# Reordering the head of a packed-attention, MoE and soft-MoE kernel, with some PSUM copies and subtractions moved to VectorE

## The chip, the cores and the metric

The kernel runs on one core of a Trainium2 chip. The metric is the device time of one execution in microseconds (us). Three timed runs of the kernel before took 532.25, 533.50 and 533.76 us; their median is 533.5 us. Five engines work side by side, each through its own queue in the order in which the program put the instructions there: PE (TensorE, matrix products), DVE (VectorE), ACT (ScalarE), POOL (GpSimd) and SP (SyncE, which here only issues DMA transfers). An instruction that waits holds up everything behind it on its own engine.

## The reference

The reference chains three layers, all in float32:

```python
# attention with 32 packed queries p per head (batch 4, 8 heads, 576 tokens, head size 64)
p_packed = softmax(scale * p @ k.T) @ v
x = softmax(scale * q @ p_packed.T) @ p_packed          # heads side by side: x is 2304 x 512
# MoE: 4 experts, hidden size 1024, weights dp = domain_probs / row sum
y = sum_e dp[:, e] * (relu(x @ w1[e]) @ w2[e])
# soft MoE: 8 experts with 4 slots each
logits = y @ phi
d, c = softmax(logits, over tokens), softmax(logits, over slots)
out = c @ [ relu((d.T @ y)[e] @ m1[e]) @ m2[e] for each expert e ]
```

## The kernel before

**What is multiplied.** The kernel never forms x or y. With `a` the second softmax of the attention (per token 8 heads times 32 packed keys, laid as 128 rows x 576 tokens for each of the two groups of heads g) and G = p_packed @ w1 (tile `g`, one 256-wide block of hidden units for two experts), the hidden layer of an expert is relu(G.T @ a): `mm1`, L477, tiles `h` and `ht`. Both factors are split into a rounded part and a rest ("hi" and "lo", type fp32r), and hi\*hi + hi\*lo + lo\*hi is accumulated: six products of 128x128 by 128x288 for each half of the tokens. The logits come straight from `ht` with wphi = w2 @ phi (L504, tile `lg`), so all of w2 has to be turned and multiplied with phi once before the first logits.

**The main loop.** There are 16 blocks n (4 batches times 4 blocks of 256 hidden units) and 8 slots for each block, one for each half block and expert. A slot runs its steps in the order F, G, L, M, S, A, P, slots 0 to 3 with M ahead of L: turn the last slot's `ht` (DVE L487) and weight it (POOL L488), now and then make the next G, the slot's `h` products and their relu (ACT L481), logits, softmax, a step of the next batch's attention, pooling. From the second batch on the attention is spread over the loop. The last third of the time streams the weights of the soft MoE and multiplies them.

**The head.** The first batch's attention and the work on w2 have no loop to hide in, and the string `HEAD` lays them out by hand: each character emits one step. `0` and `1` take the next step of the attention of head group g=0 or g=1 (generator `attention`, from one `yield` to the next), `w` the next step of `wphi_steps`, `G` makes one G block (`make_g`, L447 to L459). A `w` step turns two 128-row blocks of w2 for one expert: eight PE transposes (tile `w2t`, L255, four for each block) into one of two PSUM tiles, and a copy of each back over the weights (L260, on ACT for both since `EV` is "00"). After four such steps (one pair of blocks, "fp" 0 to 3) come 32 products with phi (tile `pw`, L241), at the start of the next `w`. The two last steps take `pw` to `wphi` (`wpt`, `wps`, L269 to L275). After the string the rest of both attentions, `norm_probs` (the row sums of domain_probs, a dozen small DVE instructions) and a second `G` follow, then slot 0; slots 0 to 3 take `WG` = 2 further `w` steps each.

**The end of an attention.** A group's softmax `nat` is turned to `a2` rows by DVE (L404), then split, twice (once for each r): ACT rounds 64 rows to "hi" (L413), and `gp` subtracts to "lo" (L414). `gp` is DVE for g=0 and POOL for g=1. `a2_t[0][0]` ("a2_00") and `a2_t[0][1]` ("a2_01") get half of their rows from each group, so the first `h` needs both groups.

**Buffers.** `h`, `g` and score tiles take four PSUM tiles in turn, `w2t` and `wps` two. In the head, g=1 takes its turned tiles ("kt") from the pool of the later `ht` tiles (4 buffers), and its `ex` and `nat` from the second half of the G buffers (`gt[1]`).

Of the kernel before, what the change touches and what calls it, by code (L numbers as in the profile page):

```python
# [9 lines left out]
F32 = mybir.dt.float32  # L10
F32R = mybir.dt.float32r
AF = mybir.ActivationFunctionType
ALU = mybir.AluOpType
# [5 lines left out]
def tile_packed_attention_moe_softmoe(  # L19
# [15 lines left out]
    pe, act, dve, pool, sp = nc.tensor, nc.scalar, nc.vector, nc.gpsimd, nc.sync  # L35

    NB, H, S, D = q.shape
# [19 lines left out]
    PIECES = ((0, 6), (6, 12), (12, 18))  # L57
    ENDS = ((0, 4), (4, 8), (8, 12), (12, 16), (16, 18))
    OFF1 = 9
    HEAD = "000101001011w1001w0011w10w0w1100w10w0101w1w1Gwww10w1G10w"  # L60
    LOADS = "PKkvaqVbQcXd1Wn2W3"
    WARM = 16
    WG = 2
    FILL = 3
    FILL_AT = 1
    EV = "00"
    GP1 = "pool"
    ORDER = "FGLMSAP"

# [83 lines left out]
    def run_due():  # L153
        todo, due[:] = due[:], []
        for f in todo:
            f()
# [67 lines left out]
    def w2_row(ft, e):  # L224
        o = DM * (2 * e + ft % 2)
        return hn_flat[:, PLACE[0][ft // 2], o : o + DM]
# [8 lines left out]
    def wphi_steps():  # L235
        pw = [ps_lg.tile([128, 512], F32, tag="lg", name=f"pw{i}") for i in range(2)]

        def project(ft):
            for dc in range(NDC):
                for e in range(NE):  # L240
                    pe.matmul(  # L241
                        pw[ft // 4][32 * e : 32 * e + 32, 128 * (ft % 4) : 128 * (ft % 4) + 128],
                        phi_sb[:, dc, :],
                        w2_row(ft, e)[:, 128 * dc : 128 * dc + 128],
                        start=(dc == 0),
                        stop=(dc == NDC - 1),
                        tile_position=(0, 32 * e),
                    )

        for fp in range(NFT // 2):  # L250
            for e in range(NE):
                for ft in (2 * fp, 2 * fp + 1):
                    ps = tr_ps(f"w2t_{ft}_{e}")
                    for dc in range(NDC):
                        pe.transpose(  # L255
                            ps[:, 128 * dc : 128 * dc + 128],
                            w2_row(ft, e)[:, 128 * dc : 128 * dc + 128],
                            ident,
                        )
                    (dve.tensor_copy if EV[ft % 2] == "1" else act.copy)(  # L260
                        w2_row(ft, e), ps
                    )
                yield
            project(2 * fp)
            project(2 * fp + 1)
        yield
        for i in range(2):
            wt = sx(f"wpt{i}", [128, 512])
            (dve.tensor_copy if i else act.copy)(wt, pw[i])  # L269
            ps = tr_ps(f"wps{i}")  # L270
            for j in range(4):
                pe.transpose(
                    ps[:, 128 * j : 128 * j + 128], wt[:, 128 * j : 128 * j + 128], ident
                )
            (act.copy if i else dve.tensor_copy)(  # L275
                wphi[:, 4 * i : 4 * i + 4, :].rearrange("p a b -> p (a b)"), ps
            )
            yield
# [3 lines left out]
    def attention(b, g, feeds, ptb, pkb, etb, tmp, gp):  # L282
# [24 lines left out]
        for h in range(4):  # L307
            r = slice(32 * h, 32 * h + 32)
            dve.transpose(
                out=ptb[r, :, 32 * h : 32 * h + 32],  # L310
                in_=pn[r].rearrange("p (j d) -> p j d", j=2),
            )
        kt = [flip(qkv_t.pop(("k", b, g, 0)), "k", 0)]
# [5 lines left out]
        for hf in range(2):  # L319
            ps = scores(ptb, kt[hf], f"sa{bg}{hf}")  # L320
# [16 lines left out]
        for hf in range(2):  # L337
            for h in range(4):
                r = slice(32 * h, 32 * h + 32)
# [40 lines left out]
        for hf in range(2):  # L380
            ps = scores(pkb, qt[hf], f"sb{bg}{hf}")
# [28 lines left out]
        for r in range(2):  # L410
            rows = slice(64 * ((r + g) % 2), 64 * ((r + g) % 2) + 64)
            hi, lo = a2_t[b][r][rows, 0], a2_t[b][r][rows, 1]
            act.copy(hi, a2[rows])  # L413
            gp.tensor_tensor(out=lo, in0=a2[rows], in1=hi.bitcast(F32), op=ALU.subtract)  # L414
        yield

    def att_tmp(tag, name):
# [353 lines left out]
    with tc.manual_schedule():  # L771
# [45 lines left out]
        pp1 = gt[0][:, :256].rearrange("p (j m) -> p j m", j=2)  # L817
        et1 = gt[0][:, 512 : 512 + 2 * S].rearrange("p (r x m) -> p r x m", r=2, m=64)
        spare = {"ex": gt[1][:, :S], "nat": gt[1][:, S : 2 * S]}
        et_x = []  # L820
        for g in range(2):
            et_x.append(a2_pool.tile([128, 2, HB, 64], F32, tag="a2", name=f"etx{g}"))
# [5 lines left out]
        load_probs()  # L828

        def head_tmp(tag, name):  # L830
            if tag == "kt":
                return ht_pool.tile([128, S], F32, tag="ht", name=name)
            return spare[tag]
# [9 lines left out]
        ng = 0  # L843
# [23 lines left out]
                pool_slots(*post.pop(0))  # L867
                limit -= 1

        for e in range(ng, 2):  # L870
            make_g(0, e)
            run_due()

        def finish_wphi():
            for _ in wgen:
# [2 lines left out]
        for sl in range(nslot + 1):  # L878
            n, r = divmod(sl, 8)
            pr, (kf, el) = r // 4, divmod(r % 4, 2)  # L880
            e = 2 * pr + el
            b, i = divmod(n, NU)
            run = sl < nslot
            if not run:
                slots.extend([(a2_pool, "a2", None)] * 2)
                slots.extend([(g_pool, "g", i) for i in range(2)])
                fill_stream()
            run_due()
            if run and b + 1 < NB:
                if sl % 32 == 0:  # L890
                    att_gens.append(start_attention(b + 1, 0))
                if sl % 32 == OFF1:
                    att_gens.append(start_attention(b + 1, 1))
            def step_attention():
                for gen in list(att_gens):
                    if next(gen, "end") == "end":
                        att_gens.remove(gen)
                        if b + 2 == NB and not att_gens and sl % 32 > OFF1:
                            att.close()
                            open_stream("s1", "right")  # L900
                if sl == (NB - 1) * NU * 8:
                    slots.extend([(a2_pool, "a2", None)] * 2)
                if sl == (NB - 1) * NU * 8 + 10:
                    assert not post
                    for k in range(NBLK // XC):
                        ring_slots(k, (0,))
                if sl % FILL == FILL_AT or sl > nslot - 8:
                    fill_stream(sp, 1)

            def step_softmax():  # L910
                nonlocal sm_gen, ready, soon
                ready += soon
                soon = 0
                if sm_gen is not None:
                    st = next(sm_gen, "end")
                    if st == "dp":
                        soon = 1
                    elif st == "end":
                        sm_gen = None

            def step_flip():
                if prev is not None:
                    flip_h(*prev)

            def step_g():
                if not run or r % 4:
                    return
                gn, ge = (n + 1, 0) if r else (n, 1)
                if sl and gn < NB * NU:
                    make_g(gn, ge)  # L930
                    if (gn, ge) == (NB * NU - 1, 1):
                        run_due()
                        slots.extend([(w1_pool, "w1", i) for i in (0, 1, 0, 1)])

            def step_mm():
                if run:
                    mm1(n, kf, e)
                    if n == NB * NU - 1 and kf == 1 and e == 1:
                        slots.extend([(g_pool, "g", i) for i in range(2)])

            def step_logits():
                nonlocal sm_gen, sm_last
                if sl < 4:
                    for _ in range(WG):
                        next(wgen, None)
                if lgq and lgq[0][0] < sl:
                    if sl == 4:
                        finish_wphi()
                    _, ln, lk = lgq.pop(0)
                    logits(ln, lk)  # L950
                    if ln == NB * NU - 1 and lk == 0:
                        sm_last = softmaxes(NB - 1)
                        next(sm_last)
                    if ln % NU == NU - 1 and lk == 1:
                        sm_gen = sm_last if ln == NB * NU - 1 else softmaxes(ln // NU)

            prev, flq = flq, (n, kf, e) if run else None
            steps = {
                "A": step_attention, "S": step_softmax, "F": step_flip, "G": step_g,
                "M": step_mm, "L": step_logits, "P": lambda: run_post(1),  # L960
            }
            for key in "FGMLSAP" if sl < 4 else ORDER if run else "LSFAP":
                steps[key]()
            if run and r % 4 == 3:
                lgq.append((sl, n, pr))
                if b and r == 3 and i == 0:
                    post.extend((b - 1, m) for m in range(len(PIECES)))
# [224 lines left out]
```

## Time and profile before

| | before |
|---|---|
| median of 3 runs | 533.5 us |
| the profiled execution's own time | 533.42 us |
| span of its instructions | 531.6 us |
| PE busy | 493.3 us (93%) |
| DVE / ACT / POOL busy | 292.7 / 236.0 / 248.3 us |
| mean granted TensorE clock | 0.976 of full |
| moved by DMA | 104.06 MB |

The profiled execution's time is 1.8 us more than the span, which runs from its first to its last instruction; it lies within the three timed runs. Times in the rows count from the start of the span. A row of a timeline tells when a group of equal instructions started, how long the group took, how many there were, and in brackets how long the engine was idle just before and who ended that. The granted clock (PEclk) is 1.00 at 2.4 GHz and 0.50 at 1.2 GHz.

### The profile page before, as it was taken

To read this page: it belongs to the slowest core of one execution; us is meant where nothing else is said; L and a number is where in the kernel's file an instruction comes from. 1 tells how busy PE (TensorE), PEld (TensorE's weight loads), DVE (VectorE), ACT (ScalarE), POOL (GpSimd) and SP (SyncE) were. 2 spreads that over 40 slices of the span, in tenths; PEclk is the share of its full clock that TensorE was granted. 3 is DMA by queue.
4 is the path that set the end of the run, shared out by engine and by line. 5 is a ranking of instruction groups with operands and counts; after the bars stand their busy time and mean duration, and the time that the engine had idled before them with its cause. 6 is when DMAs were issued, how large, how long until landed. Compare 5 with 4: busy or idle time off the path is not lost.

```text
span 531.6 us, 12920 instructions
## 1 busy us (share of the span) xinstructions
PE 493.3 (93%) x5404; PEld 349.0 (66%) x5404; DVE 292.7 (55%) x539; ACT 236.0 (44%) x539; POOL 248.3 (47%) x310
## 2 busy tenths in 40 slices
PE   6898999999999999999999999999999987998883
PEld 5776877778765677787557778865678864323232
DVE  6265566656677656567775755676554553412031
ACT  3847555664552447465424474652355430111031
POOL 8502356487752367875326567842455540300000
PEclk9899999999999999999999999999999998898996
DMA  8999135433440353443304423443359449999998
GB/s 276 367 373 315 46 103 191 161 126 127 140 144 3 106 190 105 148 157 104 104 1 150 146 82 129 150 170 109 121 187 390 173 167 373 408 408 407 373 317 282
DMA packets 66713, 104.06 MB, mean 196 GB/s; under 512 B 4368, under 2 KB 50192, under 8 KB 66656
## 3 DMA queue, kind: packets, MB, share of 16 engines
q1 hardware_dynamic: 62640, 93.10, 49.5%
q0 software_dynamic: 3232, 9.75, 6.0%
q8 instruction: 42, 0.69, 0.5%
q10 hardware_dynamic: 784, 0.39, 0.3%
q14 instruction: 15, 0.12, 0.1%
HBM read 98.52 MB, written 4.72 MB: 194 GB/s over the span
## 4 chain that ended last, share of the span: by engine, by line
PE 66%; DMA 11%; DVE 8%; ACT 8%; issue 3%; POOL 3%; SPq 1%; POOLq 0%; DVEq 0%; ACTq 0%
PE h L477 32%; PE sl L648 7%; PE lg L504 6%; PE g L447 5%; DMA ck<-in_moe_w_dram 5%; DMA hn<-in_moe_w_dram 3%; ACT etm L340 3%; PE pv L350 3%; PE sb L301 3%; PE sa L301 2%; DMA k<-in_k_dram 2%; PE w2t L255 1%; PE si L1027 1%; PE o L1153 1%; POOL hn L488 1%
## 5 line engine op out<-in xcount | busy, mean ns | idle before, releaser
L477 PE MATMUL h<-a,g 128*128 128x288 f32 x1536 | 226.2, 302 | 2.5 <-POOL a L414 1.6
L477 PEld LDWEIGHTS h<-a,g 128*128 128x128 f32 x1536 | 208.0, 188 | 28.3 <-issue 22.3
L488 POOL TENSOR_TENSOR hn<-hn,dp_sb 128x576 f32<-128x576 f32 x128 | 151.5, 1190 | 123.0 <-DVE hn L487 118.7
L481 ACT ACTIVATE ht<-h 128x288 f32<-128x288 f32 x256 | 103.7, 412 | 149.4 <-PE h L477 149.0
L487 DVE STREAM_TRANSPOSE hn<-ht 128x576 f32<-128x576 f32 x128 | 96.6, 760 | 55.1 <-ACT ht L481 55.0
L459 DVE TENSOR_TENSOR g<-g,g 128x512 fp32r<-128x512 f32 x64 | 41.1, 684 | 26.5 <-ACT g L458 26.5
L648 PE MATMUL sl<-hn,dpt 32*32 32x512 f32 x1152 | 48.1, 597 | 1.5 <-DVE dpt L607 1.2
L458 ACT CAST g<-g 128x512 fp32r<-128x512 f32 x64 | 34.3, 588 | 21.0 <-PE g L447 21.0
L504 PE MATMUL lg<-ht,wphi 128*32 128x288 f32 x512 | 37.8, 412 | 0.0
L447 PE MATMUL g<-w,gl 64*32 64x512 f32 x512 | 35.7, 601 | 0.2 <-DVE tacc L666 0.2
L648 PEld LDWEIGHTS sl<-hn,dpt 32*32 32x32 f32 x1152 | 21.0, 103 | 21.5 <-issue 11.1
L504 PEld LDWEIGHTS lg<-ht,wphi 128*32 128x32 f32 x512 | 13.5, 109 | 32.7 <-issue 25.5
L350 PE MATMUL pv<-etm,v 128*64 128x64 f32 x468 | 20.0, 232 | 7.1 <-ACT etm L340 4.0
L414 POOL TENSOR_TENSOR a<-a,a 64x576 fp32r<-64x576 f32 x14 | 19.9, 1425 | 9.6 <-ACT a L413 8.9
L350 PEld LDWEIGHTS pv<-etm,v 128*64 128x64 f32 x468 | 17.1, 144 | 11.1 <-ACT etm L340 5.7
L340 ACT COPY etm<-et 32x288 f32<-32x288 f32 x52 | 22.2, 428 | 2.4 <-DVE et L334 1.2
L1120 PE MATMUL so<-hn,tacc 128*32 128x384 f32 (+1 forms) x96 | 19.5, 487 | 2.5 <-DMA hn<-in_moe_w_dram 2.4
L382 DVE STREAM_TRANSPOSE nat<-sb 128x288 f32<-128x288 f32 x14 | 6.8, 483 | 25.4 <-PE sb L301 25.4
L255 PE MATMUL w2t<-ident,hn 128*128 128x128 f32 x128 | 19.3, 301 | 1.4 <-ACT hn L260 1.4
L666 DVE TENSOR_TENSOR tacc<-sl,tacc 128x512 f32<-128x512 f32 (+2 forms) x32 | 15.3, 544 | 9.4 <-PE sl L648 9.4
L260 ACT COPY hn<-w2t 128x512 f32<-128x512 f32 x32 | 17.4, 588 | 6.8 <-PE w2t L255 6.8
L255 PEld LDWEIGHTS w2t<-ident,hn 128*128 128x128 f32 x128 | 15.8, 154 | 5.9 <-ACT hn L260 3.8
(179 smaller groups left out, 483.6 us busy)
## 6 DMA issues: line engine op xcount, KB each, us to landing
w<-in_moe_w_dram SPq DMA_DIRECT2D x32, 1024.0 KB, 5.3
ck<-in_moe_w_dram SPq DMA_DIRECT2D x44, 512.0 KB, 8.9
hn<-in_moe_w_dram SPq DMA_DIRECT2D x40, 512.0 KB, 9.9
hn<-in_moe_w_dram SPq DMA_DIRECT2D x16, 384.0 KB, 8.4
q<-in_q_dram POOLq DMA_DIRECT2D x12, 288.0 KB, 3.2
k<-in_k_dram POOLq DMA_DIRECT2D x10, 288.0 KB, 3.3
v<-in_v_dram POOLq DMA_DIRECT2D x10, 288.0 KB, 3.2
out_dram<-ob SPq DMA_DIRECT2D x7, 384.0 KB, 4.4
```

The lines of the kernel that those rows point to most:

```text
L255: pe.transpose(ps[:, 128 * dc : 128 * dc + 128], w2_row(ft, e)[:, 128 * dc : 128 * dc + 128], ident,)
L340: act.copy(etb[hf % len(etb)][r, h % 2, :, 32 * (h // 2) : 32 * (h // 2) + 32], et[r, HB * hf : HB * hf + HB, :],)
L350: pe.matmul(pv[64 * par : 64 * par + 64, :64], vn[:, x, :], etb[hf % len(etb)][:, par, x, :], start=(hf == 0 and x == 0), stop=(hf == 1 an ...
L447: pe.matmul(pss[g][32 * ((c + 2 * g) % 4) : 32 * ((c + 2 * g) % 4) + 32, :], gl[b % 2][r, c, :], t[r, c], start=True, stop=True, tile_posi ...
L458: act.copy(hi, pss[g])
L459: dve.tensor_tensor(out=lo, in0=pss[g], in1=hi.bitcast(F32), op=ALU.subtract)
L477: pe.matmul(ps[:, :HS], gg[:, l, g, e % 2, fs], r[:, ts], start=(g == 0 and t == 0), stop=(g == 1 and t == 2),)
L481: act.activation(out=ht[:, ts], in_=ps[:, :HS], func=AF.Relu)
L487: dve.transpose(out=own, in_=unturned.pop((n, kf, e)).rearrange("p (x t) -> p x t", t=32))
L488: pool.tensor_tensor(out=own, in0=own, in1=dp_sb[:, n // NU, :, e].unsqueeze(2).to_broadcast([128, NBLK, 32]), op=ALU.mult,)
L504: pe.matmul(lg_t[b, pr][32 * c : 32 * c + 32, :HS], wphi[:, 2 * i + kf, 32 * e : 32 * e + 32], ht_t[n, kf, e][:, HS * hf : HS * hf + HS], ...
L648: pe.matmul(pss[f][c : c + 32, :], dpt[r, x, :], hn[r, p0 : p0 + NU, x, 2 * ep : 2 * ep + 2].rearrange("p n e k f -> p n (e k f)"), start= ...
```

## The change

- `HEAD`: the first step of the ending of g=0 (its casts) is emitted right after its turning (`0` instead of `w` near the end: `...w01w1Gww11w`), and the string stops earlier. The last three `w` steps of the string are left to slots 0 to 3, which take two each as before.
- The second `G` of block 0 is no longer made before slot 0 but in slot 1, in the step G, ahead of that slot's `h` products.
- Of the copies of `w2t` for w2's third pair of blocks (numbers 8 to 11 in the count 4\*fp + e, that is fp = 2), the odd block goes to DVE, the even one stays on ACT.
- The subtraction for `a2_00` is on DVE for both groups in batch 0; that for `a2_01` of g=1 stays on POOL.
- The first turned k tile of g=1 goes to a free part of `gt[1]` instead of an `ht` buffer.

```diff
-    HEAD = "000101001011w1001w0011w10w0w1100w10w0101w1w1Gwww10w1G10w"
+    HEAD = "000101001011w1001w0011w10w0w1100w10w0101w01w1Gww11w"
-    EV = "00"
+    EV_SPLIT = range(8, 12)
...
-                    (dve.tensor_copy if EV[ft % 2] == "1" else act.copy)(
-                        w2_row(ft, e), ps
-                    )
+                    split = ft % 2 and 4 * fp + e in EV_SPLIT
+                    (dve.tensor_copy if split else act.copy)(w2_row(ft, e), ps)
...
-            gp.tensor_tensor(out=lo, in0=a2[rows], in1=hi.bitcast(F32), op=ALU.subtract)
+            (dve if not b and r == 0 else gp).tensor_tensor(
+                out=lo, in0=a2[rows], in1=hi.bitcast(F32), op=ALU.subtract
+            )
...
+        spare_kt = [gt[1][:, 2 * S : 3 * S]]
...
+            if tag == "kt" and spare_kt:
+                return spare_kt.pop()
...
-        for e in range(ng, 2):
-            make_g(0, e)
-            run_due()
...
             def step_g():
+                if sl == 1:
+                    make_g(0, 1)
```

On PE the place is the stretch behind the last turning of w2's third pair of blocks (`w2t_4` and `w2t_5`). Before, in the program's order; `h0_0_0` is the first slot, `g0_1` the second G of block 0 (eight rows of it, two shown):

```order
L255 MATMUL w2t_5_3_652<-ident_103,hn_118 128x128 x4
L241 MATMUL pw1_280<-hn_118,tacc_108 32x128 x32
L255 MATMUL w2t_6_0_698<-ident_103,hn_118 128x128 x4
L255 MATMUL w2t_7_0_704<-ident_103,hn_118 128x128 x4
L447 MATMUL g0_1_0_715<-w1_0_1_166,gl0_113 32x512
L447 MATMUL g0_1_1_716<-w1_0_1_166,gl0_113 32x512
...
L255 MATMUL w2t_6_1_731<-ident_103,hn_118 128x128 x4
L255 MATMUL w2t_7_1_737<-ident_103,hn_118 128x128 x4
L477 MATMUL h0_0_0_0_757<-a2_00_660,g0_0_605 128x288 x3
L477 MATMUL h0_0_0_0_757<-a2_01_661,g0_0_605 128x288 x3
```

The same engine and place after the change:

```order
L255 MATMUL w2t_5_3_663<-ident_103,hn_118 128x128 x4
L478 MATMUL h0_0_0_0_683<-a2_00_555,g0_0_610 128x288 x3
L478 MATMUL h0_0_0_0_683<-a2_01_556,g0_0_610 128x288 x3
L478 MATMUL h0_0_0_1_691<-a2_00_555,g0_0_610 128x288 x3
L478 MATMUL h0_0_0_1_691<-a2_01_556,g0_0_610 128x288 x3
L241 MATMUL pw1_279<-hn_118,tacc_108 32x128 x32
L255 MATMUL w2t_6_0_731<-ident_103,hn_118 128x128 x4
L255 MATMUL w2t_7_0_737<-ident_103,hn_118 128x128 x4
```

The first slot's `h` now stands ahead of `pw`, of the first two experts of w2's last pair of blocks, and of the second G.

On DVE the place is between the end of g=0's attention (`a20`) and `norm_probs` (`dps`). Before:

```order
L404 STREAM_TRANSPOSE a20_539<-nat0_434 128x576
L389 TENSOR_REDUCE bm1_541<-gt1_201 128x18
L396 TENSOR_REDUCE bm1_541<-gt1_201 128x18
L397 TENSOR_SCALAR bm1_541<-bm1_541 128x18
L398 RECIPROCAL bm1_541<-bm1_541 128x18
L459 TENSOR_TENSOR g0_0_605<-g0_0_0_606,g0_0_605 128x512
L459 TENSOR_TENSOR g0_0_605<-g0_0_1_607,g0_0_605 128x512
L404 STREAM_TRANSPOSE a21_658<-gt1_201 128x576
L414 TENSOR_TENSOR a2_00_660<-a20_539,a2_00_660 64x576
L414 TENSOR_TENSOR a2_01_661<-a20_539,a2_01_661 64x576
```

The same stretch of DVE after the change, from the reduction behind `a20`'s turning:

```order
L388 TENSOR_REDUCE bm1_540<-gt1_201 128x18
L413 TENSOR_TENSOR a2_00_555<-a20_538,a2_00_555 64x576
L413 TENSOR_TENSOR a2_01_556<-a20_538,a2_01_556 64x576
L261 COPY hn_118<-w2t_5_0_600 128x512
L395 TENSOR_REDUCE bm1_540<-gt1_201 128x18
...
L460 TENSOR_TENSOR g0_0_610<-g0_0_1_612,g0_0_610 128x512
L261 COPY hn_118<-w2t_5_1_633 128x512
L261 COPY hn_118<-w2t_5_2_645 128x512
L403 STREAM_TRANSPOSE a21_651<-gt1_201 128x576
L413 TENSOR_TENSOR a2_00_555<-a21_651,a2_00_555 64x576
L261 COPY hn_118<-w2t_5_3_663 128x512
```

The subtractions of g=0 moved up, the turning of g=1 (`a21`) now stands behind three copies of `w2t_5`, and its first subtraction follows it on the same engine.

On ACT the same stretch after the change, from the exponential of g=1 (`gt1`); before, eight copies of `w2t` stood here and the casts of g=0 came after all of them:

```order
L412 CAST a2_01_556<-a20_538 64x576
L393 ACTIVATE gt1_201<-gt1_201 128x576
L261 COPY hn_118<-w2t_4_0_594 128x512
L459 CAST g0_0_610<-g0_0_0_611 128x512
L459 CAST g0_0_610<-g0_0_1_612 128x512
L261 COPY hn_118<-w2t_4_1_627 128x512
L261 COPY hn_118<-w2t_4_2_639 128x512
L412 CAST a2_00_555<-a21_651 64x576
L412 CAST a2_01_556<-a21_651 64x576
L261 COPY hn_118<-w2t_4_3_657 128x512
L482 ACTIVATE ht0_0_0_682<-h0_0_0_0_683 128x288
```

Here one copy of each pair is left, and the casts of both groups stand earlier, g=1's ahead of the last copy of this pair of blocks.

## Rows read from the trace of the kernel before

**Rows 1.** The profile page: busy us of each engine, share of the span, instructions.

```profile
PE 493.3 (93%) x5404; PEld 349.0 (66%) x5404; DVE 292.7 (55%) x539; ACT 236.0 (44%) x539; POOL 248.3 (47%) x310
```

**Rows 2.** Windows of the tail: each engine's busy us, PEclk, DMA share, GB/s.

```profile
395.00:420.00 25.00, 25.00 (x234) 20.00 (x233) 12.43 (x17) 12.60 (x29) 13.60 (x12) 1.00 0.73 274
460.00:480.00 20.00, 19.54 (x132) 6.16 (x132) 4.60 (x16) 2.40 (x6) 0.00 (x0) 0.91 1.03 409
```

**Rows 3.** Timeline of PE in the head: start us, us, work, idle before.

```profile
36.93 1.09 PE L255 MATMUL w2t<-ident,hn 128*128 128x128 f32 x8
37.95 1.09 PE L447 MATMUL g<-w,gl 64*32 64x512 f32 x16
39.41 1.15 PE L255 MATMUL w2t<-ident,hn 128*128 128x128 f32 x8 [0.36 <-ACT hn L260]
41.36 1.15 PE L255 MATMUL w2t<-ident,hn 128*128 128x128 f32 x8 [0.80 <-ACT hn L260]
42.69 1.15 PE L255 MATMUL w2t<-ident,hn 128*128 128x128 f32 x8 [0.18 <-ACT hn L260]
43.77 2.18 PE L241 MATMUL pw<-hn,tacc 128*32 128x128 f32 x64
...
49.88 0.66 PE L477 MATMUL h<-a,g 128*128 128x288 f32 x3 [0.73 <-POOL a L414]
51.37 1.54 PE L477 MATMUL h<-a,g 128*128 128x288 f32 x8 [0.82 <-POOL a L414]
52.70 3.43 PE L255 MATMUL w2t<-ident,hn 128*128 128x128 f32 x16
55.89 1.83 PE L477 MATMUL h<-a,g 128*128 128x288 f32 x12
...
62.98 0.63 PE L272 MATMUL wps<-ident,wpt 128*128 128x128 f32 x4 [0.24 <-DVE wpt L269]
...
67.11 1.18 PE L504 MATMUL lg<-ht,wphi 128*32 128x288 f32 x16
```

**Rows 4.** Windows of the head, columns as in Rows 2: PE busy comes first.

```profile
37.00:44.00 7.00, 5.65 (x55) 3.63 (x54) 3.17 (x6) 5.30 (x11) 2.31 (x2) 1.00 1.07 372
49.00:52.20 3.20, 1.65 (x11) 1.27 (x10) 2.54 (x6) 2.17 (x6) 2.24 (x2) 1.00 0.94 311
52.40:55.60 3.20, 3.20 (x17) 2.82 (x16) 3.04 (x15) 1.60 (x5) 0.00 (x0) 0.50 0.04 14
```

**Rows 5.** Timeline of ACT, same place.

```profile
38.20 0.68 ACT L394 ACTIVATE gt<-gt 128x576 f32<-128x576 f32 x1 [2.69 <-POOL gt L390]
38.79 1.06 ACT L260 COPY hn<-w2t 128x512 f32<-128x512 f32 x2
39.73 1.09 ACT L458 CAST g<-g 128x512 fp32r<-128x512 f32 x2
...
47.67 1.37 ACT L413 CAST a<-a 64x576 fp32r<-64x576 f32 x2
```

**Rows 6.** Timeline of DVE, same place.

```profile
36.15 0.71 DVE L389 TENSOR_REDUCE bm<-gt 128x18 f32<-128x576 f32 x1
38.91 0.75 DVE L396 TENSOR_REDUCE bm<-gt 128x18 f32<-128x576 f32 x1 [2.06 <-ACT gt L394]
...
40.36 1.29 DVE L459 TENSOR_TENSOR g<-g,g 128x512 fp32r<-128x512 f32 x2 [0.19 <-ACT g L458]
41.57 0.77 DVE L404 STREAM_TRANSPOSE a<-gt 128x576 f32<-128x576 f32 x1
45.06 1.54 DVE L414 TENSOR_TENSOR a<-a,a 64x576 fp32r<-64x576 f32 x2 [2.73 <-ACT a L413]
...
60.22 0.69 DVE L275 COPY wphi<-wps 128x512 f32<-128x512 f32 x1 [3.92 <-PE wps L272]
```

**Rows 7.** Timeline of POOL, same place.

```profile
48.42 2.89 POOL L414 TENSOR_TENSOR a<-a,a 64x576 fp32r<-64x576 f32 x2 [6.94 <-ACT a L413]
```

## Prediction: what bounds the head, what the change moves, and the time that follows

> **What bounds the kernel now.** I first read the busy times: PE works 493.3 of 531.6 us, no other engine more than 293 [rows 1]. The main loop is therefore PE's, and the change adds and removes no PE work, so only idle time or a slow clock can move. Then the tail: at 395 us PE is busy for all of the stretch, from 460 us on the DMA engines are at their limit (share 1.03) [rows 2]. Those transfers go into buffers that the loop gives back, so I take it that whatever the head gains or loses arrives at the end undiminished. All that is touched lies between 36.9 us (w2's third pair of blocks) and 67.1 us (the first logits): before and behind it the order is the same.
>
> In that stretch PE is idle 0.36, 0.80 and 0.18 us ahead of `w2t`, where ACT's copies are late; 0.73 and 0.82 us ahead of the first `h`, where POOL's subtraction is late; and 0.24 us ahead of `wps`: 3.13 us together [rows 3]. A second loss is the clock. From 49.0 to 52.2 us PE worked only 1.65 of 3.20 us, still at 1.00 (2.4 GHz); from 52.4 to 55.6 us it was granted 0.50 (1.2 GHz) [rows 4]. The 16 `w2t` turnings there took 3.19 us (52.70 to 55.89), where a step of eight takes 1.02 (36.93 to 37.95), two of them 2.04 [rows 3]: 1.15 us lost. So 4.28 us could be won in the best case, 0.8% of the time.
>
> **The change, step by step, at full clock.** I lay the new order over the old times, engine by engine, with the durations of the rows.
>
> *Casts of g=0 early: free.* The turning of g=0 is over by 36.2 us, since the reduction behind it starts at 36.15 [rows 6]. ACT then stands idle for 2.69 us until its exponential at 38.20, and the two casts need 1.37 [rows 5]. DVE is idle for 2.06 us until 38.91; the two subtractions take 1.54 (37.0 to 38.55), and the copy of `w2t_5_0` that now follows them some 0.69, if DVE's copy of the same size (L275) is the measure [rows 6]. That ends at 39.2: DVE's reduction comes 0.3 us late, and POOL's product with it.
>
> *Copies shared out: one better, two worse.* The first pair's wait stays (0.36): ACT's exponential ends at 38.9 and its copy at 39.4 as before [rows 3, 5]. On ACT the G casts and then one copy instead of two follow, so the next first turning starts at 40.9 instead of 41.36, idle 0.35 instead of 0.80. But its second one needs a copy on DVE, and there it stands behind the reduction, two small steps and both G subtractions. These ran from 38.91 to 41.57 [rows 6]; 0.3 later they end at 41.8, the copy at 42.45. PE has been free since 41.5: idle 0.95, which is new. Its copy in turn (43.05 to 43.8) holds the last turning to 43.85: idle 0.35 instead of 0.18. The third pair of blocks is done at 44.4; before, at 43.77 [rows 3].
>
> *The first h: earlier, but its wait is longer.* `h` now comes at once behind those turnings; `pw`, two steps of the last pair and the second G, some 5 us of work, no longer stand ahead of it. The turning of g=1 (L404, 41.57 before) waits behind three DVE copies until 43.8 and ends at 44.5 [rows 6]. Two casts of 0.68 end at 45.2 and 45.9 [rows 5]; DVE's subtraction runs 45.2 to 46.0 (half of 1.54 [rows 6]); POOL's one remaining subtraction, half of 2.89 [rows 7], from 46.0 to 47.4. PE gets its four operands at 45.25, 46.03 and 47.44 for the late ones, with 0.3 and 0.6 us of products between: idle 0.80, 0.48 and 0.79, that is 2.07 instead of 1.55. Subtracting on two engines does save a POOL step of 1.4 us and the operands are there 3.9 us earlier than 51.37 [rows 3], but `h` moved forward by more than that.
>
> *What is moved behind it* finds its operands done. The last pair's four steps keep ACT for both copies; two chained steps are 1.33 us apart (41.36 to 42.69 [rows 3]), so two waits of 0.18 remain, which the slow clock covered before. The wait ahead of `wps` (0.24) goes, since `pw` now ends a slot earlier relative to it. The second G's subtractions stand behind `norm_probs` on DVE, but they are first used in slot 4; the load that follows it on SP is issued some 6 us later and needed 10 us after the first logits, so I cost both at nothing. If that cover were gone, the cost would be a wait of a few us in slot 4. The k tile's new place costs nothing: the same turning writes to another address.
>
> The sum at full clock: idle 0.36 + 0.35 + 0.95 + 0.35 + 2.07 + 2 x 0.18 = 4.44 us against 3.13 + 1.15 = 4.28 before. That is 0.2 us more, and the slow stretch is not in it yet.
>
> **The clock.** From 44.2 to 47.4 us PE would work 0.2 + 0.3 + 0.6 = 1.1 of 3.2 us, less than the 1.65 after which it was granted half speed [rows 4]. I therefore expect one stretch at half speed here too. Its price has two ends: nothing, when it falls on PE's waits, and 1.6 us, half of a 3.2 us stretch filled with work. The row of the same kind says 1.15; since part of it may fall on the waits ahead of `h`, I take 1.0. The sum is 0.2 + 1.0 = +1.2 us on the profiled 533.42 (span 531.6 plus 1.8 around it, 0.1 under the median of the runs): **534.6 us**.
>
> The Trainium skill ("TensorE: Matmul & The Clock Gate", Part 4: PE-mode transpose) says that a transpose does not count as PE work for the clock in the way a matmul does. Here it does not agree: from 37 to 44 us PE did one G and otherwise turnings, 5.65 of 7.00 us busy, and was granted 1.00 throughout [rows 4].
>
> **Rivals.** *No slow stretch:* the waits are spread, and PE kept its full clock over 37 to 44 us although it was idle for 1.35 of 7 us [rows 4]; the waits of the third pair and of `h` may each stay above what lets it fall. Then only the 0.2 remains: 533.6 us.
>
> *Two slow stretches, slower:* the thin part is longer now, 40.4 to 47.4 us with 1.65 + 2.07 = 3.7 us of idle time, so half speed could be granted both inside it and right behind it, where `pw` and eight or sixteen turnings run. Each costs between 1.15 and 1.6 us: 533.4 + 0.2 + 2.3 to 3.2, about 536.2. It decides from the point where PE loses 1.4 us to the clock in all. I give it 0.18.
>
> *Turnings taken for idle time, slower still:* if `w2t` did not hold up the clock, half speed would be granted from the early forties on until `h` runs without waits: three stretches at 1.15 us, 533.4 + 0.2 + 3.5 = 537.1 us. The windows speak against it [rows 4], with 1.00 over a stretch of turnings: 0.03. This is what the rule of the Trainium skill named above would lead to.
>
> *The wait ahead of h goes:* this is what the new order is laid out for. If the turning of g=1 were not held up on DVE (if the copies were ready sooner than I have it), the operands would be there 1.5 to 2 us earlier, before PE asks for them; without thin stretch no half speed: 533.4 + 0.2 - 2.07 = 531.5 us. Against it stands the order on DVE, where three copies precede the turning, each bound to a PE step.
>
> *The change does not do what it says:* for g=1 the casts follow the turning, but the turning itself is late; this is part of the forecast already.
>
> **How the numbers follow.** One slow stretch 0.44; none 0.25; two 0.18, three 0.03; the wait gone 0.10. A difference under 0.3%, 1.6 us, can hardly be told from no change for this kernel. The first case spreads from 533.6 to 535.2, nearly all of it within 1.6 us; with the second it makes the same 0.68. Slower is the two and three stretches and the upper end of the first case, 0.23; faster 0.09. The range from 532.3 to 536.2 leaves out the wait-gone case and the worst of the slow ones.
>
> **What would show it.** In the profile after: `h` at L478 starting near 45.2 us instead of 48.8, with three waits on ACT, DVE and POOL of some 2 us together; a PE wait near 41.5 to 42.4 us released by a DVE copy (L261); a stretch of PEclk 0.50 that ends before 53 us; the first logits between 66.8 and 68.7 us. Logits before 66 us would make the forecast wrong, and so would a DVE copy well off 0.69 us, a wait in slot 4, or a tail that does not pass the head's difference on.

## The result, and where the profile shows it

The change makes the kernel slower by a little. The median of seven runs is 535.73 us (534.34 to 537.42) against 532.25 us (531.22 to 533.76) for the kernel before, run beside it: a ratio of 1.0063 (1.0038 to 1.0089). Run again later it gave 534.49 us against 532.95, 1.0037 (1.0022 to 1.0051). The time lies inside the range of the prediction, 1.1 us above its 534.6, but both intervals are above 1, and the first lies clear of the 0.3% that I had set as the line. I had given slower 0.23 only.

The profiled execution after took 534.34 us with a span of 532.4. The page's line of busy times answers [rows 1]; PE's work is the same 5404 matmuls.

```profile
PE 492.4 (92%) x5404; PEld 347.5 (65%) x5404; DVE 296.9 (56%) x544; ACT 234.0 (44%) x535; POOL 247.4 (46%) x309
```

PE's timeline in the head answers [rows 3] (start us, us, work, idle before and who ended it):

```profile
37.45 1.09 PE L448 MATMUL g<-w,gl 64*32 64x512 f32 x16
39.47 1.09 PE L255 MATMUL w2t<-ident,hn 128*128 128x128 f32 x8 [0.93 <-ACT hn L261]
40.93 0.66 PE L255 MATMUL w2t<-ident,hn 128*128 128x128 f32 x4 [0.37 <-ACT hn L261]
42.66 1.09 PE L255 MATMUL w2t<-ident,hn 128*128 128x128 f32 x8 [1.07 <-DVE hn L261]
44.10 0.66 PE L255 MATMUL w2t<-ident,hn 128*128 128x128 f32 x4 [0.35 <-DVE hn L261]
45.48 0.40 PE L478 MATMUL h<-a,g 128*128 128x288 f32 x1 [0.73 <-ACT a L412]
46.27 0.66 PE L478 MATMUL h<-a,g 128*128 128x288 f32 x3 [0.39 <-DVE a L413]
47.66 1.34 PE L478 MATMUL h<-a,g 128*128 128x288 f32 x8 [0.73 <-POOL a L413]
48.93 1.96 PE L241 MATMUL pw<-hn,tacc 128*32 128x128 f32 x64
...
52.15 1.14 PE L255 MATMUL w2t<-ident,hn 128*128 128x128 f32 x8 [0.24 <-ACT hn L261]
...
57.21 1.14 PE L255 MATMUL w2t<-ident,hn 128*128 128x128 f32 x8 [0.24 <-ACT hn L261]
...
67.34 1.18 PE L505 MATMUL lg<-ht,wphi 128*32 128x288 f32 x16
```

The new order is there: `h` comes at 45.48 instead of 48.77 us, with three waits, on ACT, DVE and POOL. All waits in these rows together are 5.05 us, against 3.13 in [rows 3]. Three of them stand out against the forecast: 0.93 at 39.47, 1.07 at 42.66, and 0.73 ahead of `h`.

The best ruler is the distance from the first G (37.45 here, 37.95 in [rows 3]) to the first logits, since executions differ by half a us and more before that G, where PE's order is the same in both kernels. It is 29.89 us after and 29.16 before. From the first logits to the end it is 464.1 to 465.1 us in each of the twelve traces of this study, so to within that 1 us nothing behind the head gives anything back. The second part of the answer is a second trace of the kernel before, unchanged, whose head looks like this:

```profile
37.80 1.09 PE L447 MATMUL g<-w,gl 64*32 64x512 f32 x16
39.26 1.14 PE L255 MATMUL w2t<-ident,hn 128*128 128x128 f32 x8 [0.36 <-ACT hn L260]
41.20 1.15 PE L255 MATMUL w2t<-ident,hn 128*128 128x128 f32 x8 [0.81 <-ACT hn L260]
42.54 1.14 PE L255 MATMUL w2t<-ident,hn 128*128 128x128 f32 x8 [0.19 <-ACT hn L260]
43.61 2.19 PE L241 MATMUL pw<-hn,tacc 128*32 128x128 f32 x64
...
48.62 0.38 PE L477 MATMUL h<-a,g 128*128 128x288 f32 x1
49.73 0.66 PE L477 MATMUL h<-a,g 128*128 128x288 f32 x3 [0.73 <-POOL a L414]
51.21 1.33 PE L477 MATMUL h<-a,g 128*128 128x288 f32 x8 [0.83 <-POOL a L414]
52.38 1.03 PE L255 MATMUL w2t<-ident,hn 128*128 128x128 f32 x8
53.65 1.14 PE L255 MATMUL w2t<-ident,hn 128*128 128x128 f32 x8 [0.24 <-ACT hn L260]
...
65.80 1.18 PE L504 MATMUL lg<-ht,wphi 128*32 128x288 f32 x16
```

It has the waits of [rows 3], and one of 0.24 us at 53.65 that is not in them; the turnings at 52.38 run at full clock, and the logits come 28.00 us behind the G: the half-speed stretch of [rows 4] is not there, and it was worth 29.16 - 28.00 = 1.16 us. The first trace after has no such stretch in the head either. So like against like the change costs 29.89 - 28.00 = 1.89 us. In three parts: from the G to the next turnings 2.02 instead of 1.46 (+0.56); from there to the end of the third pair of blocks, 44.76 (44.10 + 0.66) and 43.68 (42.54 + 1.14), 5.29 instead of 4.42 (+0.87); and from there to the logits 22.58 instead of 22.12 (+0.46).

The second profile of the kernel after has the same waits to 0.02 us, but a half-speed stretch behind those of `h`. Its windows, and below them those of the first profile at the same place of the program (us, PE, PEld, DVE, ACT, POOL busy, PEclk, DMA share, GB/s):

```profile
43.90:47.30 3.40, 1.72 (x8) 1.03 (x8) 2.57 (x5) 1.82 (x3) 1.26 (x1) 1.00 1.07 361
47.40:50.70 3.30, 3.20 (x28) 2.86 (x32) 3.10 (x15) 0.82 (x2) 0.04 (x1) 0.50 0.22 72
```

```profile
44.10:47.50 3.40, 1.71 (x8) 1.03 (x8) 2.57 (x5) 1.82 (x3) 1.30 (x1) 1.00 1.07 361
47.50:50.80 3.30, 3.14 (x72) 2.79 (x72) 3.10 (x15) 0.82 (x2) 0.11 (x1) 1.00 0.25 81
```

PE did 1.72 and 1.71 of 3.40 us, and then one execution was granted 0.50 and got through 28 matmuls, the other 1.00 and 72. From the G to the logits the first needs 31.30 us, 1.41 more than 29.89. What decides between them these rows don't show.

### The profile page after: what moved, and what is told of

The parts are those of the page before. It is cut to its first block, busy times and chain, and to the rows that moved or that the text cites. A ratio compares the mean times of both kernels' runs of the same rounds, so it can differ in the third digit from the quotient of the medians.

```text
span 532.4 us, 12916 instructions
## 1 busy us (share of the span) xinstructions
PE 492.4 (92%) x5404; PEld 347.5 (65%) x5404; DVE 296.9 (56%) x544; ACT 234.0 (44%) x535; POOL 247.4 (46%) x309
## 4 chain that ended last, share of the span: by engine, by line
PE 62%; DMA 16%; DVE 8%; ACT 7%; issue 3%; POOL 2%; SPq 1%; POOLq 0%; DVEq 0%; ACTq 0%
PE h L478 32%; DMA hn<-in_moe_w_dram 7%; PE lg L505 6%; PE sl L649 6%; DMA ck<-in_moe_w_dram 6%; PE g L448 5%; ACT etm L339 3%; PE pv L349 3%; PE sb L300 3%; PE sa L300 2%; DMA k<-in_k_dram 2%; PE o L1156 1%; PE w2t L255 1%; POOL hn L489 1%; PE pw L241 1%
## 5 line engine op out<-in xcount | busy, mean ns | idle before, releaser
L460 DVE TENSOR_TENSOR g<-g,g 128x512 fp32r<-128x512 f32 x64 | 41.1, 684 | 26.4 <-ACT g L459 26.4
L413 POOL TENSOR_TENSOR a<-a,a 64x576 fp32r<-64x576 f32 x13 | 18.6, 1428 | 6.6 <-ACT a L412 5.9
L255 PEld LDWEIGHTS w2t<-ident,hn 128*128 128x128 f32 x128 | 14.7, 146 | 7.1 <-ACT hn L261 3.4
L261 ACT COPY hn<-w2t 128x512 f32<-128x512 f32 x28 | 15.2, 586 | 7.7 <-PE w2t L255 7.7
```

The costliest lines, as they stand in the source:

```text
L255: pe.transpose(ps[:, 128 * dc : 128 * dc + 128], w2_row(ft, e)[:, 128 * dc : 128 * dc + 128], ident,)
L460: dve.tensor_tensor(out=lo, in0=pss[g], in1=hi.bitcast(F32), op=ALU.subtract)
```

## The experiments

In every kernel below the ruler is the same, from the first G to the first logits; the kernel before has 28.00 without and 29.16 with a half-speed stretch. Each time is the median of the runs, beside runs of the kernel before on the same chip.

**Both kernels again, unchanged.**

> The kernel before once more, unchanged. The timed runs say that the change costs some 3.4 us, the two profiled executions only 0.8 us of span. Theory 'head': the kernel before has its half-speed stretch behind the first h only in some executions; in those without it the first logits come near 66 us instead of 67.1. Theory 'elsewhere': the head is the same as in the first profile and the difference between executions sits behind 440 us, in the tail that streams weights.

532.59 us over 12 runs, 1.0001 (0.9986 to 1.0016) of the kernel before: the comparison holds to 0.15%.

> The changed kernel once more, unchanged, beside the kernel before on the same chip: ratio near 1.006. Theory 'head': the first logits come at 67.3 us where no half-speed stretch falls into the head and 1 to 2 us later where one does, and that is what its executions differ by. Theory 'elsewhere': the first logits stay within 0.3 us of 67.3 and the executions differ in the tail.

534.49 us, 1.0037 (1.0022 to 1.0051). The loss is real, and the traces of both are the ones shown above. The two comparisons of the change, +3.5 and +1.5 us, stand around what the traces give: +1.89 when neither has a stretch, 31.30 - 28.00 = +3.30 when only the kernel after has one. How many of the timed runs had one is not known: only their mean granted clock is on record, and it also takes in stretches of slow clock in the tail.

**The copies back on ACT.**

```diff
-    EV_SPLIT = range(8, 12)
+    EV_SPLIT = ()
```

> The change without its copies of w2t on DVE (all on ACT). Theory 'head, copies': the waits of 1.07 and 0.35 us on DVE's copies go, the turning of g=1 is no longer held up and the first h starts near 43.8 us instead of 45.5; its own waits shrink from 1.85 to some 1.3 us. First logits 1.4 us earlier than in the changed kernel, time about 1.4 us lower. Theory 'elsewhere': no more than 0.5 us.

532.56 us, 0.9998 (0.9990 to 1.0007): with this one term undone the loss is gone. PE's timeline (its G started at 39.42, the whole program being 2 us late by then):

```profile
41.45 1.14 PE L255 MATMUL w2t<-ident,hn 128*128 128x128 f32 x8 [0.93 <-ACT hn L261]
43.39 1.15 PE L255 MATMUL w2t<-ident,hn 128*128 128x128 f32 x8 [0.81 <-ACT hn L261]
44.72 1.15 PE L255 MATMUL w2t<-ident,hn 128*128 128x128 f32 x8 [0.18 <-ACT hn L261]
45.91 0.40 PE L478 MATMUL h<-a,g 128*128 128x288 f32 x1
...
67.73 1.18 PE L505 MATMUL lg<-ht,wphi 128*32 128x288 f32 x16
```

28.31 us from the G, 1.58 less than after. The DVE wait (1.07) and the 0.73 ahead of `h` are gone, 0.81 and 0.18 are back; only the 0.93 at the top remains as it was.

**The old order, with the copies and the subtractions as after.**

```diff
-    HEAD = "...w0101w01w1Gww11w"
+    HEAD = "...w0101w1w1Gwww10w1G10w"
...
+        for e in range(ng, 2):
+            make_g(0, e)
+            run_due()
...
-                if sl == 1:
-                    make_g(0, 1)
```

The loop makes only a G that the string has left over; with two `G` in it, as in the kernel before, it makes none. So the second G stands inside the string there, and not behind it as the section on the kernel has it; the rows of the order had it right. The two strings have 14 and 12 `w`, so the change leaves two `w` steps to the slots, and not three as the section on the change has it.

> The change without its new order of the head: the old string and the second G ahead of slot 0; DVE's copies, DVE's subtraction and the k tile's new place stay. Theory 'head, order': h again comes behind pw, two steps of w2 and the second G, starts near 49 us, and waits some 1.2 us instead of 1.85 in all, since POOL has one subtraction less; first logits 1.3 us earlier than in the changed kernel, time 1.3 us lower or more where a half-speed stretch goes too. Theory 'elsewhere': as the changed kernel within 0.5 us.

531.65 us, 0.9979 (0.9964 to 0.9994): faster than the kernel before. 64.62 - 37.42 = 27.20 us from the G, 2.69 less than after, twice the 1.3 that I had expected. PE's timeline shows why the copies on DVE do no harm here:

```profile
38.87 1.09 PE L255 MATMUL w2t<-ident,hn 128*128 128x128 f32 x8 [0.36 <-ACT hn L261]
40.33 0.66 PE L255 MATMUL w2t<-ident,hn 128*128 128x128 f32 x4 [0.37 <-ACT hn L261]
41.43 1.09 PE L255 MATMUL w2t<-ident,hn 128*128 128x128 f32 x8 [0.45 <-DVE hn L261]
42.87 0.66 PE L255 MATMUL w2t<-ident,hn 128*128 128x128 f32 x4 [0.35 <-DVE hn L261]
...
48.23 1.08 PE L478 MATMUL h<-a,g 128*128 128x288 f32 x4
50.04 1.34 PE L478 MATMUL h<-a,g 128*128 128x288 f32 x8 [0.73 <-POOL a L413]
51.22 1.03 PE L255 MATMUL w2t<-ident,hn 128*128 128x128 f32 x8
```

The same DVE copy that PE waits 1.07 us for after is waited for 0.45 us here, and `h` has a single wait of 0.73, with other work ahead of it while the turning of g=1 and its casts run. Part of the 1.07 is therefore not the copy's own: after, it stands on DVE behind the early subtractions of g=0, which are later here.

**The new order alone, on the kernel before** (the HEAD string, the removed loop and the G in slot 1).

```diff
-    HEAD = "...w0101w1w1Gwww10w1G10w"
+    HEAD = "...w0101w01w1Gww11w"
...
-        for e in range(ng, 2):
-            make_g(0, e)
-            run_due()
...
+                if sl == 1:
+                    make_g(0, 1)
```

> The kernel before with the new order of the head alone (string, casts of g=0 early, second G in slot 1); all copies on ACT, g=1's subtractions both on POOL, k tile as before. Compared with executions that have no half-speed stretch in the head (first logits of before at 65.8 us). Theory 'head, order': h starts near 44 us and waits some 2.7 us for the a operands instead of 1.6, which loses what the vanished waits give: first logits near 66.4 us, time +0.6 us, and up to 1.5 us more where a half-speed stretch follows. Rival 'copies alone': the order is harmless and the whole loss came from DVE's copies; then 0 or a gain.

534.88 us, 1.0042 (1.0024 to 1.0061). 31.34 us from the G, with two stretches at half speed, as the windows show (columns as above):

```profile
38.40:41.60 3.20, 1.46 (x18) 1.05 (x11) 2.81 (x6) 3.20 (x7) 1.16 (x1) 1.00 1.05 368
41.80:45.00 3.20, 3.20 (x16) 2.69 (x14) 3.04 (x10) 2.39 (x5) 0.47 (x1) 0.50 1.05 385
45.20:48.40 3.20, 1.58 (x10) 1.35 (x11) 3.13 (x8) 1.20 (x3) 2.15 (x2) 1.00 0.91 298
48.60:51.80 3.20, 3.20 (x58) 2.70 (x61) 1.56 (x2) 0.41 (x1) 1.56 (x2) 0.50 0.27 57
```

This is the rival with two slow stretches, in another kernel: the waits of the third pair and those of `h` are each followed by one. The waits ahead of the late `a` operands are 0.83 and 0.82, 1.65 us for the 2.7 that I had expected, beside turnings at half speed.

**The subtraction for `a2_00` on DVE alone, on the kernel before.**

```diff
-            gp.tensor_tensor(out=lo, in0=a2[rows], in1=hi.bitcast(F32), op=ALU.subtract)
+            (dve if not b and r == 0 else gp).tensor_tensor(
+                out=lo, in0=a2[rows], in1=hi.bitcast(F32), op=ALU.subtract
+            )
```

> The kernel before with one edit alone: g=1's subtraction for a2_00 on DVE instead of POOL. Theory 'head': POOL's chain ahead of the first h has one subtraction of 1.44 us instead of two, so of the two waits of 0.73 and 0.83 us one goes: first logits near 65.0 us instead of 65.8, time -0.8 us, and the stretch after which the clock can fall is nearly filled. Rival: the wait moves to the next operand in full, no change.

531.29 us, 0.9975 (0.9962 to 0.9989); 64.61 - 37.38 = 27.23 us from the G. This part of the change is a gain by itself: one of the two POOL waits ahead of `h` goes.

**The k tile's new place alone.**

```diff
+        spare_kt = [gt[1][:, 2 * S : 3 * S]]
...
+            if tag == "kt" and spare_kt:
+                return spare_kt.pop()
```

> The kernel before with one edit alone: the first turned k tile of g=1 in the free part of the G buffer. I priced it at nothing: ratio 1.000. Rival: g=1's tiles wait less for ht buffers, the head's first 36 us get up to 0.5 us shorter (the profiles of the changed kernel start the third pair of w2 blocks 0.5 us earlier), time -0.5 us.

532.45 us, 0.9993 (0.9979 to 1.0007), 65.27 - 37.29 = 27.98 us from the G: it costs nothing, as I had it.

**The waits ahead of h filled with extra work.** This kernel computes more than the one after: twelve turnings of the identity ahead of the first `h`, whose result nobody reads.

```diff
+                if sl == 0:
+                    wp = mm_ps("warm")
+                    for _ in range(12):
+                        pe.transpose(wp[:, :128], ident, ident)
```

> The changed kernel with 12 additional turnings of the unit matrix on PE ahead of the first h (extra work, nothing reads it). They need some 1.5 us and fit into the waits of 0.73, 0.39 and 0.73 us, since the last operand comes from POOL at the same time: first logits at 67.3 us as in the changed kernel's undisturbed head. Theory 'clock': executions of the changed kernel that fall to half speed behind the waits owe it to the idle PE; with PE busy there they become rare, the median falls by some 0.5 to 1 us from the changed kernel's and the scatter gets narrower. Rival 'waits alone': the half-speed stretch has nothing to do with it; no change in the median, or up to +0.5 us for the extra work.

533.91 us, 1.0029 (1.0015 to 1.0044); its trace has no half-speed stretch in the head, and `h` follows the extra work at 45.89, with the logits at 67.40 - 37.52 = 29.88 us from the G, as after (29.89). So 1.2 us of PE work fits into the waits at no cost: what holds up the head is its operands. It doesn't decide whether the filling keeps the clock up, since the trace of after that it compares with has no stretch either, and the intervals of 1.0029 and 1.0037 overlap.

**A better order: early casts, h where it was.** Against the kernel after, the copies stay on ACT, and the second G and the last pair's steps stand ahead of `h` again, as in the kernel before; the casts of both groups stay early.

```diff
-    HEAD = "...w0101w01w1Gww11w"
+    HEAD = "...w0101w01w1Gwww11wG1w"
-    EV_SPLIT = range(8, 12)
+    EV_SPLIT = ()
...
+        for e in range(ng, 2):
+            make_g(0, e)
+            run_due()
...
-                if sl == 1:
-                    make_g(0, 1)
```

> All copies on ACT, DVE's subtraction for a2_00, and the string so laid that the a operands are cast and subtracted ahead of the last w2 steps and the second G, with h behind them as in the kernel before (end of the string w01w1Gwww11wG1w). Theory 'head': the first h finds all operands and waits for nothing; first logits 1.4 to 2.0 us earlier than before (63.8 to 64.4 against 65.8), no half-speed stretch in the head in any execution, time -1.4 us or better against the median of before. The early subtractions of g=0 on DVE still run beside POOL's first subtraction and should take 2.4 instead of 1.5 us. Theory 'elsewhere': no change.

531.27 us, 0.9977 (0.9964 to 0.9991), 64.06 - 37.56 = 26.50 us from the G. `h` runs without a wait, but the 0.94 us at the top is here too.

**The same with g=0's subtractions later.** They get a step of their own (an extra `yield` behind the casts), called behind the G.

```diff
-    HEAD = "...w0101w01w1Gwww11wG1w"
+    HEAD = "...w0101w01w1Gw0ww11wG1w"
...
             act.copy(hi, a2[rows])
+            if not b and not g:
+                continue
...
         yield
+        if not b and not g:
+            for r in range(2):
+                rows = slice(64 * ((r + g) % 2), 64 * ((r + g) % 2) + 64)
+                hi, lo = a2_t[b][r][rows, 0], a2_t[b][r][rows, 1]
+                gp.tensor_tensor(
+                    out=lo, in0=a2[rows], in1=hi.bitcast(F32), op=ALU.subtract
+                )
+            yield
```

> As the kernel with the casts early, but g=0's two subtractions on DVE come one G later, after POOL's subtraction is over. If DVE and POOL slow each other when they work at once, DVE's two take 1.54 us and POOL's 1.16 us again, the wait of 0.9 us ahead of the second pair of w2t falls back to 0.36, and the first logits come 0.5 us earlier than with the casts early: -0.5 us. If they do not, both kernels are the same.

529.98 us, 0.9952 (0.9935 to 0.9968): faster than both kernels. 63.49 - 37.58 = 25.91 us from the G. PE's timeline:

```profile
37.58 1.09 PE L458 MATMUL g<-w,gl 64*32 64x512 f32 x16
39.03 1.14 PE L255 MATMUL w2t<-ident,hn 128*128 128x128 f32 x8 [0.37 <-ACT hn L261]
...
48.41 1.84 PE L488 MATMUL h<-a,g 128*128 128x288 f32 x12
50.09 1.03 PE L255 MATMUL w2t<-ident,hn 128*128 128x128 f32 x8
```

The wait at the top is 0.37 again, and the twelve `h` products go through in one run. That run took 50.09 - 48.41 = 1.68 us from its start to the next turnings; in the kernel before it took 52.38 - 48.62 = 3.76. The difference, 2.08, is all that this kernel gains on the ruler (28.00 - 25.91 = 2.09).

## Why the prediction was right in its time, and gave too little to slower

That the time lay in the range was partly luck. The change cost 1.5 to 3.5 us where I had +1.2, and the kernel before took 0.5 to 1.2 us less than the 533.4 to which I added it; the two errors go against each other.

**The casts of g=0 were not free: +0.56.** This is the first step that failed. I had DVE's subtractions at 1.54 us [rows 6] and their followers 0.3 late. DVE's and POOL's timelines after:

```profile
36.46 2.39 DVE L413 TENSOR_TENSOR a<-a,a 64x576 fp32r<-64x576 f32 x2
38.88 0.69 DVE L261 COPY hn<-w2t 128x512 f32<-128x512 f32 x1
...
40.78 1.22 DVE L460 TENSOR_TENSOR g<-g,g 128x512 fp32r<-128x512 f32 x2
41.92 0.68 DVE L261 COPY hn<-w2t 128x512 f32<-128x512 f32 x1
```

```profile
36.50 1.73 POOL L389 TENSOR_TENSOR gt<-gt,bm 128x576 f32<-128x576 f32 x1 [10.38 <-DVE bm L388]
41.01 1.16 POOL L398 TENSOR_TENSOR gt<-gt,bm 128x576 f32<-128x576 f32 x1 [2.78 <-ACT hn L261]
```

Moved to 36.46, DVE's subtractions run beside POOL's subtraction of the maximum (L389), and both engines lose: 2.39 us for the two instead of 1.54, and 1.73 instead of the 1.15 that POOL's row has at 36.86 in the second trace of the kernel before. DVE's loss is all in its second subtraction; the first, which began 0.04 us ahead of POOL's, took 0.75. The second by itself, and then ACT's exponential behind POOL's end:

```profile
37.24 1.61 DVE L413 TENSOR_TENSOR a<-a,a 64x576 fp32r<-64x576 f32 x1
```

```profile
38.26 0.68 ACT L393 ACTIVATE gt<-gt 128x576 f32<-128x576 f32 x1 [1.14 <-POOL gt L389]
```

POOL's end is what ACT's exponential waits for, and behind it stands the copy that PE needs: its exponential starts 0.81 us behind the G here (38.26 - 37.45), 0.25 in the kernel before (38.20 - 37.95 [rows 3, 5]). That is the 0.56. I had laid two engines' rows side by side with durations that each had alone. The last experiment shows the cause: with the two apart and ACT's casts still early, POOL's 1.16 and the wait of 0.37 are back, and the ruler goes from 26.50 to 25.91.

```profile
41.20 1.51 DVE L423 TENSOR_TENSOR a<-a,a 64x576 fp32r<-64x576 f32 x2
```

```profile
36.63 1.16 POOL L389 TENSOR_TENSOR gt<-gt,bm 128x576 f32<-128x576 f32 x1 [10.37 <-DVE bm L388]
```

The Trainium skill ("GPSIMD Engine Reference", 8. Key points) states that GpSimd shares its interfaces to SBUF with VectorE and contends with VectorE instructions that have two SBUF inputs. The trace agrees, and this rule belonged into the prediction.

**The copies shared out: right in kind, +0.87 instead of +0.63.** The wait on the DVE copy is there as forecast (1.07 for 0.95), its turn 0.35, the better one 0.37 for 0.35, the copy 0.69. Of the difference 0.14 stands in these waits (1.79 for 1.65); the rest is in no bracket, where the turnings run in pieces of eight and four. With the copies back on ACT the ruler is 1.58 us shorter. This term also made `h` wait for the turning of g=1, which stood behind three of these copies; with the old order, where there is work in front of `h`, the same copies cost nothing (27.20 against 27.23). The cost is thus one of the copies and the order together, and undoing either takes the loss away.

**The first h: right in kind.** It came 8.03 us behind the G (45.48 - 37.45) where I had 7.30 (45.25 - 37.95); 0.56 of the 0.73 is the first step's. Its waits are 0.73, 0.39 and 0.73, 1.85 in all for my 2.07. That the new order gains nothing because `h` moved forward by more than its operands was the reading, and it held: on the ruler the new order costs 28.31 - 27.23 = 1.08 us without the copies and 29.89 - 27.20 = 2.69 with them, the 0.56 of the early casts in both.

**What is moved behind it: right.** Two waits of 0.24 where I had two of 0.18, one of which the kernel before has too at full clock (53.65); the one ahead of `wps` is gone. Second G and k tile cost nothing: the 48 `h` products behind the first logits run without a wait in 6.64 us, before and after. The tail passes the head on, within 464.1 to 465.1 us.

**The sum at full clock was nearly right but for the first step.** My 4.44 us of waits measured 5.05; the 0.57 between 0.93 and 0.36 is nearly all of the difference. Against 3.13 that forecast +1.3 and, with the missing 0.56, gives 1.87; measured is 1.89. So close a match is partly chance: at full clock the waits of the kernel before are not 3.13 but 3.39 (its second trace, with the 0.24 at 53.65), so 1.66 of the 1.89 stands in waits and 0.23 in no bracket.

**The baseline was the second step that failed.** I set 4.44 against 4.28, counting the half-speed stretch of the profiled execution as a standing cost of the kernel before, so that only +0.2 was left. Two later traces of that order, unchanged or with the k tile alone, have no stretch in the head (28.00 and 27.98). The median of the runs, which I put beside the sum only to see that it lay 0.1 us away, came out 0.5 to 1.3 us lower over more runs. Had I kept the stretch off both sides, the forecast would have been 532.3 (533.4 less 1.15) plus 1.3, and 1.0 more with a stretch after: 533.6 to 534.6 against 532.3, which is 0.25 to 0.4% slower. By my own estimate the chance of slower would then have been near a half.

**The clock.** One stretch ending before 53 us was the likeliest case; one trace has it (47.31 to 50.73, 1.41 us, inside my 0 to 1.6), the other has none. Both the main case and the rival without a stretch are thus executions of the same program. Its mean share in the timed runs stays open.

## What to carry to other kernels

Before an instruction is moved into a gap, read what the other engines do in that gap: a duration from a row holds only beside what it ran beside, and here VectorE's subtractions with two SBUF inputs and GpSimd's subtraction made each other dearer. A change in the order should be judged against several executions of the kernel before, on a ruler between two marks of the program that brackets the change; a stretch of slow clock in the one profiled execution is no standing cost until a second one shows it. And work that is moved ahead gains only where its operands are ready: here the gain came from doing the casts early and leaving `h` where there was work in front of it.

## What the runs showed of the hardware

- **VectorE and GpSimd side by side.** A subtraction of 64x576 fp32 on VectorE took 0.75 us alone (two in 1.51 to 1.54). Of the two beside GpSimd's 128x576 subtraction the first, begun 0.04 us ahead of it, took 0.75 too and the second 1.61; GpSimd's went from 1.15 to 1.73. VectorE's subtraction for G (L460, from 40.78), one of whose inputs is in PSUM by the code, left GpSimd's product beside it at 1.16, what its subtraction of the same size takes alone.
- **The granted clock differs between executions of one program.** With the same waits, one execution was granted 0.50 for 3.4 us and the other stayed at 1.00; the price was 1.16 us in the kernel before and 1.41 in the kernel after.
- **A break in a run of matmuls costs more than the wait shown.** Twelve `h` in one run took 1.68 us; broken twice, with waits of 0.73 and 0.83, they took 3.76, which is 0.52 more than run and waits together. The weight loads of the two held products waited 2.0 us for GpSimd by the second trace of the kernel before, nearer to the 2.08 that the breaks cost. Taking away the wait of 0.73 alone gained 0.77 on the ruler, and 2.09 went with both.
